# Eighteen products of constants and a new order of issue for a fused attention and expert kernel

## The chip, the cores and the metric

One core of one Trainium2 chip. The metric is the device time of one execution in microseconds (us); the median of three runs counts. The engines are named as in the profile: PE (TensorE, matrix products), DVE (VectorE), ACT (ScalarE), POOL (GpSimd), SP (SyncE, which issues DMAs). Each works through its own queue in order.

## The reference, cut to what matters

Attention over keys and values that are averaged in groups of eight, and after it a layer of eight experts, of which each row of the result goes to one:

```python
k_p = k.reshape(B, H, Sp, pool, D).mean(axis=3)       # B = H = 8, S = 576, pool = 8, D = 64
v_p = v.reshape(B, H, Sp, pool, D).mean(axis=3)
attn = softmax(scale * q @ k_p.T)
x = (attn @ v_p).transpose(0, 2, 1, 3).reshape(B, S, H * D)
...
for b in range(B):                                    # x: (8, 576, 512), F = 1024
    for s in range(S):
        fresh_e = argmax(x[b, s] @ w_gate)
        e = fresh_e if s == 0 or sigmoid(x[b, s] @ w_local) < 0.5 else prev_e
        out[b, s] = p[e] * (relu(x[b, s] @ w1[e]) @ w2[e])
```

## The kernel before

Everything up to the first blocks of the expert layer is one static sequence of small steps, written out in three lists, `PLAN`, `PLAN_B` and `PLAN_C`. A token such as `sc:4` is a step and the number of the unit, load or block it works on; `do` (in the printed code below) turns it into instructions, in the order of the lists. As each engine's queue is in order, the lists fix every engine's order, and the order of SP's DMAs too.

Attention works on four pairs of batches, five units each (`units`, 20 in all). The tokens:

- `lk`, `lv`, `lq` issue the loads of keys, values and queries on SP. There are three buffers for keys (`kk`), three for values (`vt_in`), four for queries (`qt`). `kp` sums groups of eight keys on DVE. `vp` sums values, on POOL or with `.d` on DVE, `vt` transposes them on PE, `vc` copies the transpose (ACT), `vl` multiplies it with the gate weights (PE), `vd` and `vm` write the results into the tile `vaug` (DVE; `vm` on POOL, with `.d` on DVE).
- `sc` is a unit's scores (PE, L458 and L464, for the fifth unit of a pair L473); the tile `sp` has one buffer. `mx`, `sb` are row maxima and the subtraction (DVE, L487, L490), `ex` the exponential (ACT).
- `T0` to `T2` transpose the weights on PE (L521), `T0c` to `T2c` copy them out (ACT); `v0` to `v2` are the products with `vaug` (PE, L563), `v0c` to `v2c` their copies. `fs` scales the logits (DVE), `fp` and `fd` the two halves of the rows, each on POOL or DVE (L600), after which `fd` stores them.
- Per pair, `rA`, `rT0` to `rP` choose the expert of each row: small operations on DVE, transposes and small products on PE (L642, L656 to L677), scans on DVE (L647). Then nine `s` scatter row numbers by expert (POOL, L699).
- `ch`, `er` choose the expert with the most rows after two pairs; its weights are loaded (`w1`, `w2`) and split into two parts (`p1`, `p2`: ACT, then DVE with `.d`, else POOL, L211 and L216). `il` loads a block's row numbers, `ga` gathers the rows (DVE, then POOL), `XR`, `X0`, `X1` turn them.
- `PLAN_B`: `L1` and `L2` are the products of a block's two layers (PE, eight and three products each), `h0`, `h1` what lies between (ACT and DVE, L333 to L339), `tb` a table of the blocks that follow (DVE), `M1` and `M2` the same two layers for the next block. `i1`, `i2`, `i3` load row numbers (SP), `g1`, `f1`, `f3` reduce them (DVE, L256 and L297), `f2`, `f4` gather. `es`, `so` scale and store a block.
- PE writes transposes into the tile `tp` of the pool `ps_t`, which has two buffers. `wa` is three products of the identity, written before the kernel's first data is there.

After `PLAN_C` comes code with branches, `l1_two`, `rest` and `blocks`, with the same instructions before and after the change.

Of the kernel before, what the change touches and what calls it, by code (L numbers as in the profile page):

```python
# [54 lines left out]
PLAN = plan("""
lk:1 lk:0 lv:0 vp:0 lv:1 lq:0 kp:0 lk:2 lv:2 lv:5 lc:0 vm:0 vp:1 wa:0 vt:0 vc:0 kp:1 vp.d:2 sc:0 wa:1 vt:1 lk:3 mx:0
lv:3 vl:0 vt:2 vm:2 vm:1 vp:5 vc:2 vt:5 vd:0 vl:2 sb:0 vd:2 vc:1 vp:3 lq:2 ex:0 lv:6 kp:2 kp:3 lq:1 vl:1 vd:1 vm:3
vc:5 T0:0 vp:6 sc:2 T1:0 T0c:0 v0:0 mx:2 lv:4 lk:5 sb:2 vm:5 T1c:0 vt:3 v0c:0 vc:3 lv:9 v1:0 vp:4 vp:9 lv:8 T2:0 T2c:0
vp:8 vl:3 lq:3 sc:1 ex:2 vd:3 lk:4 lk:6 T0:2 vl:5 vt:4 lv:7 kp:5 lv:11 vc:4 vt:6 vm:6 v2:0 mx:1 v1c:0 lv:10 vd:5 vc:6
T0c:2 T2:2 sb:1 lq:5 v2c:0 fs:0 T1:2 vm:4 T1c:2 v0:2 kp:4 sc:3 kp:6 lq:4 lk:9 vm:8 v0c:2 vt:8 vl:4 fp:0 vd:4 ex:1 vc:8  # L60
T0:1 v1:2 lk:7 T2c:2 v1c:2 T0c:1 vl:6 v2:2 T1:1 T2:1 mx:3 v2c:2 sb:3 lk:10 fd:0 T1c:1 T2c:1 vp:7 ex:3 v0:1 lv:14 T0:3
sc:4 v0c:1 T1:3 fs:2 v1:1 v2:1 T0c:3 vd:6 mx:4 vp:10 T2:3 T1c:3 fp:2 vl:8 vp:11 lv:12 sb:4 kp:7 v1c:1 vt:10 vc:10
v2c:1 sc:5 T2c:3 lq:6 vm:11 kp:10 ex:4 lv:17 mx:5 fd.p:2 vt:7 T0:4 vd:8 fs:1 vc:7 v0:3 v1:3 v0c:3 v2:3 sb:5 lq:7 lk:11
vm:10 vm:9 vm:7 T1:4 fp:1 vl:7 T0c:4 v1c:3 T1c:4 kp:9 vt:11 fd.p:1 lq:12 vd:7 vt:9 vc:11 ex:5 sc:6 T0:5 vp:12 v2c:3
T0c:5 vl:11 mx:6 v0:4 T2:5 vp:17 v0c:4 sb:6 vc:9 v0:5 lv:16 v1:4 T1:5 lq:8 T1c:5 vp:14 v1c:4 fs:3 sc:7 kp:11 vd:11
lv:13 ex:6 fp:3 v1:5 T2c:5 vt:12 T0:6 fd.p:3 vl:9 T0c:6 vc:12 v0c:5 v1c:5 T1:6 lv:19 fs:4 T1c:6 T2:6 rA:0 v2:5 vd:9
rT0:0 mx:7 lk:12 rS0:0 vl:10 sb:7 rT1:0 T2c:6 v2c:5 lq:10 rS1:0 vm:14 fp:4 rT2:0 fs:5 vp:13 ex:7 vd:10 fd.p:4 sc:8
fp:5 lq:9 lk:8 rS2:0 vm:12 mx:8 T2:7 v0:6 T0:7 rE:0 lv:15 rL:0 T0c:7 sb:8 v0c:6 v1:6 v1c:6 T1:7 v2:6 fd.p:5 rO:0 sc:9
rR:0 T2c:7 rV:0 kp:8 T1c:7 vp:19 vt:13 pf:0 ex:8 v2c:6 v0:7 lq:11 vc:13 vp:16 T0:8 mx:9 rP:0 T0c:8 sb:9 vm.d:17 vt:14
vl:12 lv:18 lk:13 v1:7 vd:12 vc:14 vp:15 T1:8 T2:8 sc:10 vm.d:13 ex:9 fs:6 mx:10 lk:15 v0c:7 lq:14 T1c:8 s:0 T0:9 fp:6  # L70
T2c:8 fd.p:6 v1c:7 vl:14 v2:7 v2c:7 v0:8 T0c:9 v0:9 vd:14 vt:15 sb:10 lq:16 s:0 v0c:8 T1:9 T1c:9 vc:15 fs:7 lv:20
sc:11 ex:10 v1:8 v1c:8 s:0 lv:21 s:0 fp:7 T0:10 vm.d:15 vl:13 kp:13 mx:11 kp:12 v2:8 v2c:8 vd:13 v1:9 T1:10 lk:14
vl:15 lq:13 sb:11 vp:18 sc:12 T1c:10 fd.p:7 v0c:9 T2:10 v1c:9 vd:15 fs:8 kp:15 T0c:10 s:0 v0:10 vt:17 ex:11 T2c:10
vc:17 mx:12 sb:12 fp:8 T1:11 fd.p:8 vp:21 T2:11 fs:9 v1:10 T1c:11 vl:17 vm:16 s:0 s:0 rA:1 lv:23 v0c:10 vt:16 v2:10
v1c:10 vc:16 v2c:10 vd:17 fs:10 s:0 T0:11 T2c:11 T0c:11 sc:13 rT0:1 ex:12 rT1:1 rS0:1 vl:16 vd:16 v0:11 vp:20 rS1:1
vt:20 mx:13 rT2:1 rS2:1 fp:9 fp:10 lq:15 rE:1 vc:20 fd.p:10 sb:13 v1:11 rL:1 T1:12 T0:12 T1c:12 s:0 v1c:11 vt:18
v0c:11 rO:1 rR:1 sc:14 vc:18 rV:1 T0c:12 rP:1 v2:11 T2:12 ch:0 vl:18 ex:13 fd.p:9 v0:12 v0c:12 mx:14 lq:19 s:0 kp:14
er:0 s:0 T0:13 v2c:11 vm:21 T2c:12 T0c:13 sb:14 v1:12 T1:13 w2:0 s:0 vt:19 v1c:12 T1c:13 fs:11 vd:18 vp.d:23 w1:0
v2:12 v2c:12 T2:13 s:0 vm:20 s:0 T2c:13 v0:13 lv:22 sc:15 ex:14 fs:12 fp.d:11 vm.d:19 vl:20 fd:11 s:0 w1:1 lq:17 vd:20
fp:12 v1:13 s:0 T1:14 v0c:13 s:0 mx:15 v2:13 sb:15 vc:19 vm.d:23 p1.d:0 vl:19 T0:14 v1c:13 sc:16 v2c:13 vm.d:18 T1c:14  # L80
ex:15 T0c:14 fd.p:12 fs:13 vt:21 vt:23 mx:16 vc:23 vc:21 v0:14 T1:15 T1c:15 vd:19 T0:15 s:0 fp:13 v0c:14 w2:2 v1:14
vl:21 T2:15 v1c:14 fd.p:13 sb:16 sc:17 fs:14 ex:16 vd:21 T0c:15 il:0 rA:2 ga:0 lq:18 p1.d:1 vp:22 T2c:15 vl:23 T2:16
v0:15 rT0:2 rT1:2 mx:17 sb:17 T2c:16 v0c:15 v1:15 vm:22 T0:16 w2:3 rS0:2 v2:15 T0c:16 rT2:2 rS1:2 v1c:15 w1:2 sc:18
rS2:2 fp.d:14 vt:22 vd:23 p2.d:0 fd:14 XR:0 X1:0 rE:2 v2c:15 vc:22 fs:15 fp:15 p2:2 T1:16 vl:22 vd:22 T1c:16 mx:18
v0:16 v1:16 X1c:0 rL:2 ex:17 T0:17 v0c:16 v1c:16 v2:16 sb:18 rO:2 w1:3 T0c:17 il:1 v2c:16 T1:17 sc:19 T2:17 rR:2 fs:16
v0:17 mx:19 T1c:17 rV:2 fd.p:15 fp:16 T2c:17 ex:18 rP:2 v0c:17 T0:18 v1:17 T0c:18 sb:19 fd.p:16 s:0 s:0 T1:18 v2:17
s:0 p1.d:3 v1c:17 T1c:18 T2:18 v2c:17 ex:19 s:0 fs:17 T2c:18 w2:1 fp.d:17 fd:17 s:0 v0:18 T0:19 v0c:18 T0c:19 v1:18
p1.d:2 v1c:18 X0:0 v2:18 X0c:0 T1:19 v2c:18 fs:18 T1c:19 v0:19 v0c:19 v1:19 v1c:19
""")
# [1107 lines left out]
```

## Time and profile before

| | us |
|---|---|
| timed, median of three runs | 643.26 (640.04 to 644.61) |
| profiled execution | 647.41 |
| its span, first to last instruction | 645.6 |
| busy in it: PE | 605.9 (94%) |
| DVE | 433.5 (67%) |
| ACT | 271.0 (42%) |
| POOL | 241.2 (37%) |

The span is made of attention up to about 180 us, the static blocks up to about 238 us, and the blocks with branches after that. Busy times are unions over an engine's instructions; matrix products are pipelined, so two of them overlap in the rows, and a product's start minus that of the one before it is what it costs in a row of products. [...]

### The profile page before, as it was taken

How to read it: one execution, taken by the hardware profiler on the slowest of the kernel's cores; microseconds unless marked ns; L12 is line 12 of the kernel's file. 1: busy time of each engine (PE TensorE's matmuls, PEld its weight loads, DVE VectorE, ACT ScalarE, POOL GpSimd, SP SyncE). 2: the span in 40 equal slices, each digit the busy share in tenths (PEclk: the TensorE clock that was granted, in tenths of full speed). 3: DMA queues.
4: the chain of work that ended last, by engine and by line, in shares of the span. 5: the costliest groups of instructions: out<-in, count | busy, mean ns of one | idle time of the engine just before them, and what ended most of it. 6: DMA issues, size and time to landing. Idle time of an engine off the chain costs nothing. (4 is left out here: it accounts for less than half of the span.)

```text
span 645.6 us, 11811 instructions
## 1 busy us (share of the span) xinstructions
PE 605.9 (94%) x3588; PEld 513.6 (80%) x3588; DVE 433.5 (67%) x1004; ACT 271.0 (42%) x612; POOL 241.2 (37%) x295
## 2 busy tenths in 40 slices
...
GB/s 308 369 291 318 297 271 214 70 268 183 119 67 2 118 298 195 169 101 115 133 75 311 145 112 247 206 192 292 314 174 109 133 58 336 279 200 132 77 82 61
DMA packets 74964, 120.10 MB, mean 186 GB/s; under 512 B 21486, under 2 KB 42994, under 8 KB 74868
## 3 DMA queue, kind: packets, MB, share of 16 engines
...
## 5 line engine op out<-in xcount | busy, mean ns | idle before, releaser
L326 PE MATMUL hp<-x,w1h 128*128 128x512 f32 x376 | 134.5, 398 | 0.0
L347 PE MATMUL o_ps<-w2h,ht_l 128*128 128x512 f32 x312 | 122.5, 392 | 2.4 <-DVE ht_l L339 2.4
L347 PE MATMUL o_ps<-w2h,ht_h 128*128 128x512 f32 x312 | 123.3, 395 | 1.5 <-PEq L1127 0.9
L347 PE MATMUL o_ps<-w2l,ht_h 128*128 128x512 f32 x312 | 121.9, 391 | 1.1 <-DVE w2l L216 1.1
L305 POOL DMA_INDIRECT kk<-x_rows,mi x44 | 44.1, 1003 | 191.1 <-DVE mi L301 172.3
L328 PE MATMUL hp<-x,w1l 128*128 128x256 f32 x376 | 105.6, 281 | 0.0
L333 ACT COPY hs<-hp 128x256 f32<-128x256 f32 x94 | 34.7, 371 | 147.0 <-PE hp L328 145.7
L326 PEld LDWEIGHTS hp<-x,w1h 128*128 128x128 f32 x376 | 70.6, 188 | 17.4 <-DVE hs L334 0.3
L563 PE MATMUL op<-vaug,aT 128*128 128x148 f32 (+5 forms) x448 | 71.6, 321 | 1.7 <-ACT osb L372 1.7
L328 PEld LDWEIGHTS hp<-x,w1l 128*128 128x128 f32 x376 | 71.0, 189 | 1.2 <-DVE w1l L211 0.4
L347 PEld LDWEIGHTS o_ps<-w2h,ht_l 128*128 128x128 f32 x312 | 58.7, 188 | 16.5 <-DVE ht_l L339 3.2
L338 ACT ACTIVATE ht_h<-hs 128x256 fp32r<-128x256 f32 x136 | 56.9, 420 | 34.2 <-DVE hs L334 31.0
L347 PEld LDWEIGHTS o_ps<-w2h,ht_h 128*128 128x128 f32 x312 | 58.8, 189 | 14.6 <-ACT ht_h L959 2.0
L563 PEld LDWEIGHTS op<-vaug,aT 128*128 128x128 f32 (+1 forms) x448 | 65.2, 191 | 6.5 <-ACT osb L372 2.4
L347 PEld LDWEIGHTS o_ps<-w2l,ht_h 128*128 128x128 f32 x312 | 58.9, 189 | 12.7 <-DVE w2l L216 1.4
L339 DVE SCALAR_TENSOR_TENSOR ht_l<-hs,ht_h 128x256 fp32r<-128x256 f32 x136 | 56.7, 417 | 3.4 <-ACT ht_h L338 3.0
L1062 POOL DMA_INDIRECT out<-ob,mi x22 | 28.2, 1284 | 76.2 <-DVE ob L1059 28.3
L334 DVE TENSOR_TENSOR hs<-hp,hs 128x256 f32<-128x256 f32 x94 | 38.7, 418 | 25.9 <-ACT hs L333 24.9
L1059 DVE TENSOR_SCALAR ob<-o_ps,ms 128x512 f32<-128x512 f32 x22 | 16.5, 749 | 51.5 <-PE o_ps L347 49.6
L699 POOL DMA_INDIRECT ids<-pm,pos x36 | 38.0, 1054 | 19.4 <-DVE pos L696 10.9
L1062 POOL DMA_INDIRECT out<-vt_in,mi x20 | 22.5, 1125 | 59.3 <-DVE vt_in L1059 19.3
L319 ACT CAST x<-qt 128x512 fp32r<-128x512 f32 x40 | 24.0, 611 | 42.7 <-DVE qt L314 42.7
...
## 6 DMA issues: line engine op xcount, KB each, us to landing
...
```

Source lines behind the costliest of these rows:

```text
L305: nc.gpsimd.indirect_dma_start(out=xg[b % 2][:, h, :], out_offset=None, in_=x_rows[0:NT + 1], in_offset=bass.IndirectOffsetOnAxis(ap=mi[b ...
L319: nc.scalar.copy(out=xt[:, cs, 0, :], in_=xr_t[:, cs, :])
L326: nc.tensor.matmul(out=ps, lhsT=W1[0][:, kk, f * P:(f + 1) * P], rhs=xt[:, kk].rearrange("p i n -> p (i n)"), start=(kk == 0), stop=False, ...
L328: nc.tensor.matmul(out=ps[:, 0:2 * P], lhsT=W1[1][:, kk, f * P:(f + 1) * P], rhs=xt[:, kk, 0, :], start=False, stop=(kk == KD - 1), skip_g ...
L333: nc.scalar.copy(out=hb[:, 0, :], in_=ps[:, 2 * P:])
L334: nc.vector.tensor_tensor(out=hb[:, 1, :], in0=ps[:, 0:2 * P], in1=hb[:, 0, :], op=ALU.add)
L338: nc.scalar.activation(out=ht[0][:, f, :], in_=hb, func=AF.Relu)
L339: nc.vector.scalar_tensor_tensor(out=ht[1][:, f, :], in0=hb, scalar=0.0, in1=ht[0][:, f, :].bitcast(F32), op0=ALU.max, op1=ALU.subtract)
L347: nc.tensor.matmul(out=to[h], lhsT=ht[i][:, kk, h * P:(h + 1) * P], rhs=W2[j][:, kk, :], start=(n == 0), stop=(n == 3 * KF - 1))
L563: nc.tensor.matmul(out=out, lhsT=lhs, rhs=rhs if len(out.shape) == 3 else rhs.rearrange("p s x -> p (s x)"), start=all(x[0] != n for x in ...
L699: nc.gpsimd.indirect_dma_start(out=ids[u % 4].rearrange("t m w -> (t m) w"), out_offset=bass.IndirectOffsetOnAxis(ap=pos[:, u:u + 1], axis=0),
L1062: nc.gpsimd.indirect_dma_start(out=outv, out_offset=bass.IndirectOffsetOnAxis(ap=mi[b % NM][:, h:h + 1], axis=0), in_=ob[b % 2][:, h, :], ...
```

## The change

A step `wf` (`fill`) is added: one fp32 product of a 128 by 128 tile of ones with 256 columns of ones, into a buffer of `tp` that nobody reads. Eighteen stand in the new `PLAN`. All three lists are replaced. They hold the same steps as before, in another order; eight of them, from `g1` to `M2:1` and `L2:15`, move from `PLAN_C` to `PLAN_B`, and `p2:3` from `PLAN_B` to `PLAN`. Some steps change their engine between DVE and POOL.

```diff
 PLAN = plan("""
-lk:1 lk:0 lv:0 vp:0 lv:1 lq:0 kp:0 lk:2 lv:2 lv:5 lc:0 vm:0 vp:1 wa:0 vt:0 vc:0 kp:1 vp.d:2 sc:0 wa:1 vt:1 lk:3 mx:0
-lv:3 vl:0 vt:2 vm:2 vm:1 vp:5 vc:2 vt:5 vd:0 vl:2 sb:0 vd:2 vc:1 vp:3 lq:2 ex:0 lv:6 kp:2 kp:3 lq:1 vl:1 vd:1 vm:3
-vc:5 T0:0 vp:6 sc:2 T1:0 T0c:0 v0:0 mx:2 lv:4 lk:5 sb:2 vm:5 T1c:0 vt:3 v0c:0 vc:3 lv:9 v1:0 vp:4 vp:9 lv:8 T2:0 T2c:0
-vp:8 vl:3 lq:3 sc:1 ex:2 vd:3 lk:4 lk:6 T0:2 vl:5 vt:4 lv:7 kp:5 lv:11 vc:4 vt:6 vm:6 v2:0 mx:1 v1c:0 lv:10 vd:5 vc:6
...
-vl:21 T2:15 v1c:14 fd.p:13 sb:16 sc:17 fs:14 ex:16 vd:21 T0c:15 il:0 rA:2 ga:0 lq:18 p1.d:1 vp:22 T2c:15 vl:23 T2:16
...
+wa:0 lq:0 lk:1 wf:0 kp:1 lv:0 lk:0 wf:1 wf:2 vp:0 lv:1 wf:3 wf:4 wf:5 wa:1 vp:1 wf:6 vm:0 kp:0 wf:7 wf:8 lv:2 vp.d:2
+wf:9 sc:0 vt:0 lq:2 lc:0 mx:0 lv:5 vp:5 vc:0 sb:0 wf:10 lk:3 wf:11 lv:3 vt:2 lv:4 vt:1 vc:2 wf:12 vl:0 sc:2 vd:0 lv:6
+vl:2 lk:2 vc:1 wf:13 lq:1 vm.d:1 vm.d:2 kp:3 ex:0 vd:2 T0:0 T2:0 vp:3 vl:1 vm:5 lv:8 T2c:0 vd:1 vp:6 mx:2 T1:0 T0c:0
+sb:2 v0:0 T1c:0 wf:14 kp:2 v1:0 ex:2 vt:6 vm.d:3 lv:7 vt:3 vc:6 lk:5 sc:1 vp:4 vp:8 vp:7 lq:3 vm:4 mx:1 vc:3 v1c:0
...
+kp:5 T1c:2 fp:0 lk:6 wf:15 T2:2 sc:3 v1:2 ex:1 vm:7 T2c:2 v0c:2 vc:4 vl:4 T0:1 vp:9 mx:3 v2:2 sb:3 T0c:1 lq:6 v1c:2
...
+lq:8 lv:15 wf:17 v1:4 mx:6 T2:5 vp:14 vl:9 T1c:5 sb:6 T2c:5 lk:10 lv:16 v0c:4 vm:10 v1c:4 kp:11 fs:4 sc:7 ex:6 vt:10
+vd:9 vp:12 T0:6 fp:4 vc:10 fd.p:4 fp:3 lq:9 T0c:6 v0:5 T2:6 vp:15 T2c:6 mx:7 pf:0 vl:10 T1:6 vt:12 rA:0 T1c:6 v1:5
+sb:7 v0c:5 vc:12 rT0:0 vm:12 rS0:0 v2:5 fd:3 v1c:5 rT1:0 rS1:0 rT2:0 v2c:5 rS2:0 sc:8 rE:0 lv:17 ex:7 vd:10 rL:0 kp:9
+T1:7 rO:0 T0:7 fs:5 v0:6 rR:0 T1c:7 lq:11 mx:8 sb:8 rV:0 v0c:6 T0c:7 rP:0 T2:7 vm:14 v1:6 vm:15 lv:18 vm:13 vt:14 ex:8
...
+T1:14 s:0 vc:20 p1.d:0 vl:20 v2c:13 fs:13 vm:18 T0:14 T0c:14 sc:16 ex:15 T1c:14 T1:15 vd:20 s:0 w1:1 fd.p:12 wf:18
+vl:19 T1c:15 mx:16 T0:15 sb:16 T0c:15 vt:21 il:0 fp:13 vd:19 fd:13 p2.d:2 v0:14 vc:21 v1:14 vt:23 v0c:14 w2:3 v1c:14
+vl:21 T2:15 vd:21 sc:17 fs:14 ex:16 vc:23 T2c:15 ga:0 vp:22 rA:2 T0:16 v0:15 rT0:2 T0c:16 mx:17 v0c:15 rT1:2 sb:17
...
 PLAN_B = plan("""
...
-h0:6 s:0 h0:7 tb:6 tb:7 L2:11 s:0 fd:18 s:0 h1:6 s:0 fd:19 s:0 h1:7 L2:12 i2:0 L2:13 L2:5 M1:0 p2.d:3 i1:0 M1:1 M1:2
-L2:14 M1:3 f1:0 L2:6 f2:0 M1:4 L2:7 i3:0 qr:2
...
+fp.d:19 L1:7 L2:11 h0:7 L2:4 h1:6 L2:5 fd:19 X1:1 h1:7 X0c:1 L2:6 L2:12 X1c:1 fd:18 L2:7 es:1 M1:0 M1:1 so:1 i1:0 M1:2
+g1:0 i2:0 f1:0 L2:13 M2:0 f2:0 M2:1 L2:14 L2:15 i3:0 M1:3 f0:0 YR:0 qr:2 M1:4
 """)
 PLAN_C = plan("""
-es:1 g1:0 M1:5 M2:0 M2:1 f3:0 f4:0 ld:0 L2:15 M2:2 M1:6 M1:7 YR:0 es:0 M2:3 M2:4 so:1 M2:5 M2:6 Y1:0 M2:7 so:0 Y0:0
-M2:8 e1:0 M2:9 M2:10 qr:3 M2:11 M2:12 M2:13 i4:0 f0:0 M2:14 M2:15
+es:0 M1:5 M1:6 f3:0 so:0 M2:2 ld:0 f4:0 M1:7 M2:3 M2:4 M2:5 M2:6 i4:0 Y0:0 M2:7 e1:0 Y1:0 M2:8 M2:9 qr:3 M2:10 M2:11
+M2:12 M2:13 M2:14 M2:15
 """)
...
+        def fill():
+            tp = ps_t.tile([P, 512], F32, name="tp")
+            nc.tensor.matmul(out=tp[:, 0:2 * P], lhsT=ones, rhs=ones[:, 0:1].broadcast_to([P, 2 * P]), start=True, stop=True)
...
+            elif op == "wf":
+                fill()
```

## Rows read from the trace of the kernel before

**Rows 1.** Windows: us, busy us (x instructions) per engine, PEclk, DMA share, GB/s
```profile
28.00:66.00 38.00, 36.81 (x360) 33.03 (x360) 33.23 (x67) 20.93 (x54) 28.93 (x45) 1.00 0.90 309
...
82.00:140.00 58.00, 53.42 (x505) 47.93 (x503) 54.82 (x140) 30.19 (x78) 40.91 (x47) 0.97 0.59 189
...
180.00:238.00 58.00, 52.33 (x269) 42.51 (x268) 37.43 (x148) 19.96 (x50) 26.45 (x26) 0.97 0.33 96
238.00:645.60 407.60, 395.70 (x1961) 330.82 (x1959) 245.09 (x479) 163.40 (x348) 90.63 (x83) 1.00 0.53 172
```
**Rows 2.** Windows inside single stretches of the granted clock, columns as above (PE first)
```profile
10.00:27.50 17.50, 16.34 (x88) 14.27 (x89) 10.72 (x19) 3.36 (x9) 15.79 (x25) 1.00 1.04 350
...
72.20:78.90 6.70, 6.19 (x35) 5.68 (x36) 4.75 (x13) 1.66 (x5) 4.94 (x7) 0.50 0.73 256
...
157.60:164.20 6.60, 5.81 (x23) 5.64 (x24) 4.95 (x13) 4.06 (x8) 6.09 (x6) 0.50 0.72 223
...
229.30:232.50 3.20, 3.08 (x12) 2.53 (x12) 0.69 (x1) 1.39 (x3) 1.49 (x2) 0.50 0.97 237
```
**Rows 3.** Timeline of PE: start us, us, line, operation, shapes, count [idle before]
```profile
1.53 1.65 PE L746 MATMUL rt<-ident 128*128 128x128 f32 x6 [1.53 <-POOL ident masks.py:199]
...
10.62 1.17 PE L458 MATMUL sp<-kdz,qt 128*128 128x144 f32 x4
11.72 2.84 PE L464 MATMUL sp<-kd,qt 64*128 64x72 f32 x24
...
62.73 1.56 PE L464 MATMUL sp<-kd,qt 64*128 64x72 f32 x24
...
77.01 2.32 PE L563 MATMUL op<-vaug,aT 128*128 128x148 f32 x8
...
84.80 1.34 PE L563 MATMUL op<-vaug,aT 128*128 128x148 f32 x8
```
**Rows 4.** DVE to 32 us: waits (us, times, longest), then its timeline
```profile
DVE vaug L433 <- PE rt L425: 3.3, 2, 2.3
DVE vs L385 <- DMA vt_in<-in_v: 3.2, 1, 3.2
DVE mx L487 <- PE sp L464: 2.2, 2, 2.0
...
31.94 1.42 DVE L487 TENSOR_REDUCE mx<-sp 128x12 f32<-128x864 f32 x2
```
**Rows 5.** Timeline of DVE where it waits, 66 to 82 us and at 150 us
```profile
76.86 1.42 DVE L487 TENSOR_REDUCE mx<-sp 128x12 f32<-128x864 f32 x2 [1.85 <-PE sp L464]
...
81.08 0.29 DVE L666 TENSOR_TENSOR oh<-rt,iota 128x72 f32<-128x72 f32 x1 [1.46 <-PE rt L661]
...
150.15 0.18 DVE L256 TENSOR_REDUCE idm<-idn 128x4 f32<-128x16 f32 x1 [2.10 <-DMA idn<-ids]
```
**Rows 6.** Waits of PE, then of DVE, 180 to 240 us: us, times, longest
```profile
PE o_ps L347 <- DVE ht_l L339: 2.4, 1, 2.4
PE tp L642 <- DVE ab L627: 1.3, 1, 1.3
PE o_ps L347 <- DVE w2l L216: 1.1, 1, 1.1
...
DVE ids L297 <- DMA idp<-ids: 7.0, 2, 4.5
```
**Rows 7.** Timeline, 205 to 240 us: SP's first index load, DVE's last wait for one, block 0's scaling
```profile
212.56 3.11 SPq L293 DMA_DIRECT2D idp<-ids  x4
...
225.97 0.26 DVE L297 TENSOR_REDUCE ids<-idp 128x16 f32<-128x64 f32 x1 [4.51 <-DMA idp<-ids]
...
238.16 0.75 DVE L1059 TENSOR_SCALAR ob<-o_ps,ms 128x512 f32<-128x512 f32 x1 [3.40 <-PE o_ps L347]
```
**Rows 8.** Timeline of DVE, 194 to 196.5 us: one split, one half of rows
```profile
194.17 1.22 DVE L216 TENSOR_TENSOR w2l<-vt_in,w2h 128x1024 fp32r<-128x1024 f32 x1
...
195.93 0.69 DVE L600 TENSOR_TENSOR xs<-osb,rr 128x512 f32<-128x512 f32 x1
```

More of the change, by code (lines that the diff above doesn't have):

```diff
@@ L61 @@
[L61 to L80, printed above, removed]
```

36 lines of the change are left out of this document (25 added, 11 removed).

## Prediction

> **What bounds the kernel now.** I read the busy times by stage first. From 238 us to the end PE is busy 395.7 of 407.6 us [rows 1]: that part is bound by PE itself, its code isn't touched, and it is shifted as a whole. What can change is the moment at which the last M2 product of the static part ends, now just ahead of 238.16 us, where DVE's scaling of block 0 stops waiting for it [rows 7]. Before that, two stages are nearly full: PE is busy 36.8 of 38 us from 28 to 66 us, and DVE 54.8, PE 53.4 of 58 us from 82 to 140 us. The loss is at the edges: in the first 28 us, around the routing steps of each pair, and in the static block, 180 to 238 us, where PE is busy 52.3 of 58 us [rows 1].
>
> Second, the granted clock. The windows show 0.50, the 1.2 GHz level, in 72.2 to 78.9, 157.6 to 164.2 and 229.3 to 232.5 us [rows 2]. The column reads 1.00 for 10 to 27.5 us too, but the durations contradict it: 24 score products that take 1.56 us at 62.7 took 2.84 us at 11.7 [rows 3]. So I read 10 to 27.5 us as the 1.2 GHz level as well. PE was busy 16.3 us there [rows 2]; at 2.4 GHz up to half of it, 8.2 us, falls away.
>
> Third, who waits at the front. Up to 32 us DVE stands 3.2 us for a load and 3.3 and 2.2 us for PE [rows 4], 8.7 us in all, and after that it is one of the two full engines. PE's half rate delays work that can't be caught up later.
>
> [...]
>
> **The change, term by term.** Both plans hold the same steps but for `wf`, of which the diff has 18 (0 to 15, 17 and 18), not nineteen.
>
> *Price of a fill.* No row has one. Eight v records of 148 columns took 2.32 us at half level and 1.34 us at full [rows 3]. A fill is one fp32 product, two such records of 256 columns: 2 × 256/148 × 2.32/8 = 1.00 us at half level, 0.58 us at full. The lower bound is zero, where PE waits anyway.
>
> *Front (wf:0 to wf:14 and the early tokens).* wa:0 ends at 1.53 + 1.65 = 3.18 us, and PE does almost nothing until sc:0 at 10.62 us [rows 3]. Into that gap go ten fills and wa:1. Ahead of 79 us, where the level was full again, PE had run v products for 2 us [rows 2, 3], and the first six fills are a run of that kind, with 128 rows. [...] sc:0's inputs still come in about as now: lk:0 moves from second to fourth in the queue, but kp:1 goes ahead of kp:0 on DVE, so DVE has work until it lands. [...] sc:2 stands five PE steps earlier, runs at full level too, and vt:3 no longer follows a half-rate v0:0, so most of the 5.5 us of DVE's waits on PE go; lv:2 lies behind five large loads instead of six. I take 4.0 of the 8.7 us. Bounds: +8.2; and if the level never rises, ten fills at 1.00 and 1.65 for wa:1 put sc:0 at 14.8 us, −4.2.
>
> *Routing of pair 0.* In 66 to 82 us DVE waits 1.85 us for sc:8 at half level and 1.46 us for the products of rL:0 [rows 5]. The new order puts v2:5 between rT0 and rT1, T1:6, vt:12 and v1:5 ahead of rT0, and kp:9 on DVE ahead of rO:0, so each side has work while the other's is under way. I take 2.5 of 3.3 us; bounds 0 and 3.3.
>
> *First gather.* ga:0 stood 2.10 us on DVE for the rows of il:0 [rows 5]. il:0 now goes out 20 tokens ahead of ga:0 instead of two. That wait goes, and with it perhaps the low level that follows, whose 5.8 us of PE work cost 2.9 us extra [rows 2]. I take 2.0; bounds 0 and 5.0. Late next is rT1:2, behind rT0:2 and DVE's scan.
>
> *Static block.* PE waits 2.4, 1.3 and 1.1 us, and the low level after the 2.4 costs half of 3.1 us [rows 2, 6]: 6.3 us. es:1, so:1, g1, M2:0, M2:1 and L2:15 move ahead of M1:3, and p2:3, for which the 1.1 us were, leaves this stretch. Against it, i1 and i2 now stand directly before g1 and f1, which need them, so DVE stands there, and behind it wait M1:3's operations, for whose buffer M1:6 waits. Cover on PE between M1:2 and M1:6: L2:13 to L2:15, M2:0, M2:1 and M1:3 to M1:5, 39 products at 52.33/269 = 0.195 us [rows 1], 7.6 us. The index loads take from 212.56 us (issue) to 225.97 us (third used) now [rows 7], two of them about 9 us. fd:18 and fd:19 go out ahead of i1 in either order. I take 3.5, a little over half; bounds −7.3 (under C) and 6.3.
>
> *Engine moves.* Four vm and three fp go to DVE and as many away from it, fd six to it and two away, p2 one and two: 4 × 0.69 − 1.22 = +1.5 us on DVE [rows 8], hidden in DVE's waits at the front, where the vm ones land; if not, −1.5. Loads that change places I cost at nothing, behind the buffers that wait full; if not, the 3.2 us of the one load wait again.
>
> *Later fills, unknown waits.* wf:15 and wf:17 fall where PE is full: −1.2 us. wf:18 falls near 140 us, ahead of a stretch with waits: 0, or −0.6. Any order has waits of its own; 82 to 140 us lose 4.6 us of PE now [rows 1], and I charge about half as new, −2.5; bounds ±4.6.
>
> Sum: 4.0 + 2.5 + 2.0 + 3.5 − 1.2 − 2.5 = 8.3 us. The profiled execution took 647.41 us around its span of 645.6; the median of the three timed runs, 643.26, is 4.2 below. So 639.1 us if profiled in the same way, and 643.26 − 8.3 = **635.0 us** as timed.
>
> **Rivals.**
> *A: loads bind the front.* The DMA share is 1.04 in 10 to 27.5 us [rows 2], so DVE may trade waits on PE for waits on loads. Against: one DVE wait there is on a load, 3.2 us [rows 4]. Front term 0: 8.3 − 4.0 = 4.3, 639.0 us. Chance 0.18.
> *B: the fills don't do what they say,* and the level stays at 1.2 GHz until v0:0. For: wa:0, 1.65 us of full-height products, did not raise it. Against: the fills run on for 5 us. Front −4.2 instead of +4.0: 0.1, 643.2 us. Chance 0.10.
> *C, the other side: DVE stands on the index loads.* If i1 waits for the last scatter and DVE stands the 13.4 us of all three loads [rows 7] against 7.6 us of cover, M1:6 is 5.8 us late, and a low level after it adds 1.5 as at 229 us [rows 2]. It decides as soon as f1 ends more than 7.6 us after M1:2. 8.3 − 3.5 − 5.8 − 1.5 = −2.5, 645.8 us. For: f1 and f3 stood 7.0 us for such loads [rows 6]. Against: i3 has five PE steps more of cover. Chance 0.17.
>
> **How the numbers follow.** The forecast has 0.55. A measurement of this kernel can tell about 1%, 6.4 us, from no change. The forecast's own range is 628 to 641 us; 0.45 of its chance lies below 636.8, 0.10 above. A splits into 0.05 faster and 0.13 within, as other terms may run to their bounds; B is within; C gives 0.06 within and 0.11 slower, where it meets the lower bound of the front. Faster 0.50, same 0.39, slower 0.11. 627.5 to 645.0 us leaves about 2 in 10 out.
>
> **What would show it.** Right: the score products of sc:0 near 1.6 us; mx:1 starting near 28 instead of 31.94 us [rows 4]; no DVE wait over 1 us for idn ahead of 160 us; the last M2 product near 230 us, and 407 us behind it. Wrong: sc:0 still at 2.84 us (B); DVE waits for vt_in or kk in the first 40 us (A); PE idle for several us ahead of M1:6 (C); new low stretches of the clock between 82 and 180 us.

## The result and the profile after

| | before | after |
|---|---|---|
| timed, median | 641.65 (639.86 to 644.61, 4 executions) | 632.46 (631.25 to 633.65, 4 executions) |
| profiled execution | 647.41 | 631.25 |
| its span | 645.6 | 629.1 |

The ratio is 0.985, with a 95% interval of 0.980 to 0.990: 9.2 us less. Measured again later, the same changed kernel took 636.50 us (633.57 to 639.64, 12 executions) and the kernel before, beside it, 642.23, a ratio of 0.992 (0.989 to 0.995). Over everything timed the medians are 642.39 us (74 executions of before) and 635.90 us (16 of after): 6.5 us, 1.0%. The two medians of the changed kernel lie 4.0 us apart, so a difference between two kernels that weren't timed side by side is uncertain by as much, and the readings below heed that.

The windows of the changed kernel, with the columns of [rows 1]:

```profile
28.00:66.00 38.00, 36.15 (x348) 32.22 (x346) 36.87 (x83) 21.73 (x59) 33.18 (x49) 1.00 1.01 369
82.00:140.00 58.00, 52.67 (x507) 46.00 (x504) 55.64 (x143) 30.23 (x76) 40.97 (x49) 1.00 0.67 225
165.00:222.00 57.00, 54.50 (x297) 44.16 (x297) 38.20 (x153) 20.81 (x52) 30.00 (x29) 0.98 0.35 99
222.00:629.10 407.10, 395.46 (x1960) 330.68 (x1958) 244.90 (x479) 163.13 (x348) 85.54 (x81) 0.99 0.54 174
```

The last line is that of [rows 1] again, 395.5 of 407 us on PE: what was gained lies ahead of 222 us. From 28 to 66 us DVE has gone from 33.2 to 36.9 busy microseconds of 38, and the DMA share from 0.90 to 1.01.

The timeline of PE at the front of the changed kernel, with the columns of [rows 3]:

```profile
1.52 1.65 PE L747 MATMUL rt<-ident 128*128 128x128 f32 x6 [1.52 <-POOL ident masks.py:199]
2.97 4.78 PE L751 MATMUL tp<-ones 128*128 128x256 f32 x12
7.59 0.83 PE L747 MATMUL rt<-ident 128*128 128x128 f32 x6
8.25 1.90 PE L751 MATMUL tp<-ones 128*128 128x256 f32 x8
9.99 0.65 PE L459 MATMUL sp<-kdz,qt 128*128 128x144 f32 x4
10.58 1.56 PE L465 MATMUL sp<-kd,qt 64*128 64x72 f32 x24
```

The first fills start 0.85 us apart. `wa:1` takes half of what `wa:0` took, the fills behind it start 0.43 us apart, and the 24 score products take 1.56 us, where [rows 3] had 2.84. So PE runs at full clock from about 7 us on, and `sc:0` starts 0.6 us earlier than before. Full and half clock are 1.00 and 0.50 of the column PEclk, which gives the granted clock as a share; the trace holds shares alone, so the 1.2 and 2.4 GHz of the prediction are names of these two levels, and no run shows a frequency.

DVE in the changed kernel: its longest waits up to 30 us, then rows of its timeline that answer to [rows 4, 5, 7].

```profile
DVE vs L386 <- DMA vt_in<-in_v: 1.4, 1, 1.4
DVE mx L488 <- PE sp L465: 1.4, 1, 1.4
DVE kd L399 <- DMA kk<-in_k: 1.0, 1, 1.0
...
26.96 1.42 DVE L488 TENSOR_REDUCE mx<-sp 128x12 f32<-128x864 f32 x2 [1.39 <-PE sp L465]
...
137.35 0.18 DVE L257 TENSOR_REDUCE idm<-idn 128x4 f32<-128x16 f32 x1
...
206.03 0.27 DVE L298 TENSOR_REDUCE ids<-idp 128x16 f32<-128x64 f32 x1 [4.30 <-DMA idp<-ids]
...
222.00 0.75 DVE L1066 TENSOR_SCALAR ob<-o_ps,ms 128x512 f32<-128x512 f32 x1 [4.04 <-PE o_ps L348]
```

`mx:1` stands at 26.96 us, 5.0 us ahead of [rows 4]; the wait of `ga:0` is gone; block 0's scaling starts 16.2 us earlier than in [rows 7]. Behind the front, one stretch ahead of the last M2 product is at half clock. Before had four: the three of [rows 2] and one from 106.3 to 109.7 us that the prediction missed. The one that is left lies between 82 and 180 us, where the prediction looked for new ones; before had two there. The windows, first of the changed kernel, then of before:

```profile
164.10:167.40 3.30, 3.30 (x17) 2.57 (x19) 2.45 (x7) 2.39 (x5) 2.83 (x3) 0.50 0.73 294
...
106.30:109.70 3.40, 3.40 (x19) 3.14 (x18) 3.32 (x6) 1.50 (x4) 3.24 (x4) 0.50 0.55 191
```

### The profile page after: what moved, and what is told of

It is laid out like the page before. It is cut to its first block, busy times and chain, and to the rows that moved or that the text cites. A ratio compares the mean times of both kernels' runs of the same rounds, so it can differ in the third digit from the quotient of the medians.

```text
span 629.1 us, 11909 instructions
## 1 busy us (share of the span) xinstructions
PE 600.2 (95%) x3624; PEld 508.2 (81%) x3624; DVE 435.7 (69%) x1006; ACT 270.5 (43%) x612; POOL 236.9 (38%) x293
## 5 line engine op out<-in xcount | busy, mean ns | idle before, releaser
L348 PEld LDWEIGHTS o_ps<-w2h,ht_h 128*128 128x128 f32 x312 | 58.6, 188 | 14.5 <-ACT ht_h L966 2.5
L564 PE MATMUL op<-vaug,aT 128*128 128x148 f32 (+4 forms) x448 | 67.4, 313 | 0.5 <-ACT osb L373 0.5
L348 PEld LDWEIGHTS o_ps<-w2l,ht_h 128*128 128x128 f32 x312 | 58.6, 188 | 11.3
L564 PEld LDWEIGHTS op<-vaug,aT 128*128 128x128 f32 (+1 forms) x448 | 61.0, 182 | 4.8 <-issue 1.9
L340 DVE SCALAR_TENSOR_TENSOR ht_l<-hs,ht_h 128x256 fp32r<-128x256 f32 x136 | 56.8, 417 | 3.3 <-ACT ht_h L339 2.5
L335 DVE TENSOR_TENSOR hs<-hp,hs 128x256 f32<-128x256 f32 x94 | 38.8, 418 | 29.2 <-ACT hs L334 28.3
L1066 DVE TENSOR_SCALAR ob<-o_ps,ms 128x512 f32<-128x512 f32 x22 | 16.5, 748 | 52.5 <-PE o_ps L348 51.7
L1069 POOL DMA_INDIRECT out<-ob,mi x22 | 24.7, 1122 | 73.9 <-DVE ob L1066 33.8
L1069 POOL DMA_INDIRECT out<-vt_in,mi x20 | 22.5, 1127 | 63.7 <-DVE vt_in L1066 23.8
L700 POOL DMA_INDIRECT ids<-pm,pos x36 | 38.8, 1078 | 17.5 <-DVE pos L697 9.2
```

Source lines behind the costliest of these rows:

```text
L335: nc.vector.tensor_tensor(out=hb[:, 1, :], in0=ps[:, 0:2 * P], in1=hb[:, 0, :], op=ALU.add)
L340: nc.vector.scalar_tensor_tensor(out=ht[1][:, f, :], in0=hb, scalar=0.0, in1=ht[0][:, f, :].bitcast(F32), op0=ALU.max, op1=ALU.subtract)
L348: nc.tensor.matmul(out=to[h], lhsT=ht[i][:, kk, h * P:(h + 1) * P], rhs=W2[j][:, kk, :], start=(n == 0), stop=(n == 3 * KF - 1))
L564: nc.tensor.matmul(out=out, lhsT=lhs, rhs=rhs if len(out.shape) == 3 else rhs.rearrange("p s x -> p (s x)"), start=all(x[0] != n for x in ...
L700: nc.gpsimd.indirect_dma_start(out=ids[u % 4].rearrange("t m w -> (t m) w"), out_offset=bass.IndirectOffsetOnAxis(ap=pos[:, u:u + 1], axis=0),
L1069: nc.gpsimd.indirect_dma_start(out=outv, out_offset=bass.IndirectOffsetOnAxis(ap=mi[b % NM][:, h:h + 1], axis=0), in_=ob[b % 2][:, h, :], ...
```

## The experiments

All start from the changed kernel or from the kernel before; a time without a further word is a median over 6 or 12 executions, and the ratio is to the kernel before, timed side by side.

**Two runs without a change.**

> The kernel before, profiled once more. The two profiled executions differ by 16.5 us in span (645.6 and 629.1), the timed medians by 9.2 us. Theory (the low stretches of PE's clock fall differently from execution to execution, and the first profile of the kernel before had more of them than most): span 638 to 642 us with fewer low stretches than four behind 28 us. Rival (a profiled execution of the kernel before is always that long): 645 us and the same four stretches.

The kernel before, profiled again: 639.71 us, span 638.0, `mx:1` at 32.38 us, `L1:0` at 174.03, the last M2 product at 230.02 (179.69 and 237.28 us in the first profile), and two stretches at half clock behind the front instead of four, as the theory had it. So 7.6 of the 16.5 us between the first two profiles' spans lie between two executions of one kernel.

> The changed kernel as it is, beside which the other three are read. Theory: 632 to 633 us at the median, 0.985 of the kernel before; its low stretches lie elsewhere than in the first profile, since they move from execution to execution. The product with the row constants of the routing (lgx, 0.3 us when nothing disturbs it) again takes about 2.9 us near 157 us, because the same split runs on POOL beside it. Rival: that long lgx was an accident of the first execution; then it takes 0.3 us here and L1:0 comes about 2.5 us earlier than 162.8 us.

636.50 us (633.57 to 639.64), ratio 0.992; the profile has `mx:1` at 29.42 us, `L1:0` at 171.67 and the last M2 product at 228.66. The time misses the 632 to 633 us of the theory. So neither first profile may stand for its kernel, and I read all profiles together, by stage. A column is the time from one milestone to the next: starts of units' row maxima on DVE (`mx`), and of `L1:0` and `M2:15` on PE. In brackets stand the microseconds of it at half clock, by the trace's records of the granted clock; the time ahead of the first record counts as half clock, as the durations there say.

| profile | 0 to mx:6 | to mx:11 | to mx:18 | to L1:0 | to M2:15 |
|---|---|---|---|---|---|
| before | 57.4 (27.8) | 42.7 (6.8) | 61.2 (7.2) | 18.4 (3.0) | 57.6 (3.4) |
| before again | 57.8 (27.8) | 37.2 (0) | 62.1 (3.1) | 16.9 (0.3) | 56.0 (3.4) |
| before + ten fills | 54.5 (15.2) | 42.8 (6.8) | 60.2 (2.4) | 17.3 (1.0) | 56.1 (6.8) |
| before + new blocks | 55.1 (22.7) | 42.9 (6.8) | 60.9 (0) | 16.6 (0) | 58.3 (6.8) |
| after | 52.2 (7.1) | 37.9 (0) | 58.1 (0) | 20.2 (3.4) | 52.7 (0) |
| after again | 56.8 (13.9) | 38.0 (0) | 58.2 (0) | 18.7 (0) | 57.0 (6.8) |
| after, no fills | 53.6 (22.1) | 36.8 (0) | 59.2 (0) | 20.4 (3.4) | 55.8 (6.8) |
| after, ten fills | 53.8 (15.1) | 37.6 (0) | 58.1 (0) | 20.2 (3.4) | 56.1 (3.4) |
| after, front fills | 54.9 (7.9) | 38.8 (6.8) | 59.1 (0) | 20.1 (3.4) | 56.2 (6.8) |
| after, narrow fills | 55.0 (27.0) | 38.2 (0) | 58.8 (3.4) | 18.7 (0) | 57.3 (10.2) |
| after, old blocks | 53.1 (7.6) | 38.2 (0) | 58.3 (0) | 18.6 (0) | 56.9 (3.4) |
| split on DVE | 52.8 (4.6) | 38.8 (0) | 58.6 (0) | 17.2 (0) | 53.7 (0) |
| split later | 52.6 (4.5) | 37.0 (0) | 59.3 (3.4) | 16.1 (0) | 56.5 (3.4) |
| split later, loads ahead | 52.4 (5.5) | 40.8 (10.2) | 58.7 (6.8) | 16.0 (0) | 54.1 (0) |

Two columns follow their brackets. In the old order, 37.2 us from `mx:6` to `mx:11` becomes 42.7 to 42.9 where 6.8 us of it are at half clock. And the static block takes 52.7 to 54.1 us in the three profiles without a stretch at half clock, and 55.8 to 58.3 in the eleven with one. Such stretches differ between two executions of one kernel, so a single profile can't tell an order's gain from them.

**The fills.** Taken out of the changed kernel (here and below the first line of the list stands for all):

```diff
-wa:0 lq:0 lk:1 wf:0 kp:1 lv:0 lk:0 wf:1 wf:2 vp:0 lv:1 wf:3 wf:4 wf:5 wa:1
+wa:0 lq:0 lk:1 kp:1 lv:0 lk:0 vp:0 lv:1 wa:1
```

> The changed kernel with all eighteen products of constants taken out; the three lists keep their new order otherwise. Theory (the fills raise PE's clock early, and that is the front gain): sc:0 runs at the 1.2 GHz level again (24 score products in about 2.84 us instead of 1.56), mx:1 starts at 30 to 32 us instead of 27.0 us, and the time is 3 to 5 us above the changed kernel's 632.5 us, about 636.5 us. Rival 1 (the order alone does it; PE would leave the low level early in the new order anyway): within 1 us of 632.5 us, mx:1 near 27 us. Rival 2 (the fills only cost their places in PE's queue): 1 to 3 us faster than 632.5 us.

635.32 us (631.6 to 637.93), ratio 0.989 (0.983 to 0.994). The 24 products of `sc:0` took 2.84 us, the granted clock was 0.50 from 8.4 to 25.5 us, and `mx:1` came at 29.36 us, a little better than the theory's 30 to 32. But without fills the changed order is as good as with them within what these runs can tell. Alone, ten of them behind `wa:0` of the kernel before:

```diff
-vp:1 wa:0 vt:0
+vp:1 wa:0 wf:0 wf:1 wf:2 wf:3 wf:4 wf:5 wf:6 wf:7 wf:8 wf:9 vt:0
```

> The kernel before with ten fills behind wa:0 and nothing else changed: PE idles there anyway. Theory (level early is worth 4 to 5 us in any order): sc:0's 24 products take 1.56 us, mx:1 starts near 29 us instead of 31.9 us, and the time is 2 to 4 us below the 641.7 us of the kernel before. Rival (loads bind the front in the old order, or DVE does): the products are faster, yet mx:1 keeps its place and the time is within 1 us of 641.7 us.

640.98 us (636.56 to 644.42), ratio 0.997 (0.994 to 1.001). The level did rise, and fell again. PE's timeline and the windows of this kernel:

```profile
2.97 5.50 PE L751 MATMUL tp<-ones 128*128 128x256 f32 x20
10.25 0.33 PE L420 MATMUL tp<-ident,vs 128*128 128x128 f32 x1 [1.78 <-POOL vs L381]
...
11.01 2.15 PE L465 MATMUL sp<-kd,qt 64*128 64x72 f32 x24
...
11.80:22.00 10.20, 8.40 (x45) 6.84 (x43) 7.52 (x13) 2.61 (x7) 8.96 (x15) 0.50 1.04 368
```

After the ten fills PE stood 1.78 us for POOL, and from 11.8 to 22 us the granted clock was 0.50. `mx:1` came at 29.02 us, 3 us earlier than in before, but `mx:11` at 97.33 us, between the 100.06 and 95.04 of the two profiles of before. The same first list without fills had `mx:1` at 29.68 us in another run below, with the level up at 22.7 us instead of 27.8, so those 3 us aren't clear of what differs between executions. Then the fills with 8 columns in place of 256, so that PE gets as many instructions but little work:

```diff
-nc.tensor.matmul(out=tp[:, 0:2 * P], lhsT=ones, rhs=ones[:, 0:1].broadcast_to([P, 2 * P]), ...)
+nc.tensor.matmul(out=tp[:, 0:8], lhsT=ones, rhs=ones[:, 0:8], ...)
```

> The changed kernel with each product of constants cut from 256 columns to 8: all eighteen keep their places in PE's queue and their tp buffers, but hardly occupy the engine. Theory (what counts is that they keep PE occupied until its clock is granted in full): as without fills, 635.3 us, with sc:0's 24 products at 2.84 us and mx:1 near 29.4 us. Rival (their places in the queue, which hold later products back, do it): as the changed kernel, 632.5 us.

637.63 us (632.72 to 643.15), ratio 0.990 (0.985 to 0.995). The 24 products of `sc:0` took 2.84 us, and the first stretch at full clock began at 27.0 us, as the theory had it; `mx:1` came at 30.32 us. PE's timeline:

```profile
2.97 2.57 PE L751 MATMUL tp<-ones 128*128 128x8 f32 x12
6.81 1.71 PE L751 MATMUL tp<-ones 128*128 128x8 f32 x8
10.32 2.84 PE L465 MATMUL sp<-kd,qt 64*128 64x72 f32 x24
```

So narrow products in the same places leave the front at half clock up to 27.0 us, and the wide ones lift it at 7.1 us, in the first profile of the changed kernel. Yet even here the stage up to `mx:6` takes 55.0 us, where the kernels with wide fills and the new first list span 52.2 to 56.8. The later fills, left out by threes and by eights (`wf:15`, `17`, `18`; then all from `wf:10` on):

```diff
-kp:5 T1c:2 fp:0 lk:6 wf:15 T2:2 sc:3
+kp:5 T1c:2 fp:0 lk:6 T2:2 sc:3
```

> The changed kernel without wf:15, wf:17 and wf:18. Forecast's pricing (two of them fall where PE is full and cost 0.58 us each): 1 us faster, 631.5 us. Rival (they hold the clock level later on): 1 to 2 us slower, with more low stretches behind 28 us. Rival (hidden in waits of PE): no difference.

636.02 us (632.6 to 639.2), ratio 0.988 (0.984 to 0.993).

> The changed kernel with the first ten products of constants only, those ahead of sc:0. In the old order ten fills ahead of sc:0 raised the clock at 5 us, but it fell again at 11.8 us, inside sc:0, and the time gained 1.4 us at most. Theory (wf:10 to wf:14, between the first small products, hold the level until the v products come): the level falls again between 10 and 20 us, mx:1 starts near 28.5 us instead of 27.0, and the time is 1 to 2 us above 632.5 us. Rival (the new order is dense enough after sc:0): as the changed kernel.

637.78 us (632.06 to 641.65), ratio 0.993 (0.989 to 0.997). Neither can be told from the changed kernel's 636.50 us. In the profile of the ten, PE was at half clock again from 15.1 to 25.3 us, as in the kernel with the fills alone (11.8 to 22.0). In the seven profiles that have wide `wf:10` to `wf:14` too, it stayed, once up, at full clock to 27.6 us or longer: the theory was right about the clock, and the time doesn't show it.

**The order of the static block.** The changed first list with the old second and third (less `p2.d:3`, which the first list holds, and one `s:0` more):

```diff
-L1:0 fs:19 rA:3 L1:2 L1:1 h0:0 s:0 p2.d:1 rT0:3 ...
+s:0 ga:1 L1:0 fs:19 L1:2 L1:1 h0:0 rA:3 h1:0 ...
```

> The changed kernel with the old order of the static blocks, the second and third list (without p2.d:3, which is done earlier now, and with one more scatter, which the first list leaves over). Theory (the new order of the blocks saves about 4 us, as 53.5 instead of 58.4 us from the first L1 product to the last M2 product): 636 to 637 us, and that stretch takes 57 to 58 us again with PE waiting about 2.4 us for ht_l ahead of M2:5. Rival (the stretch is shorter only because the steps ahead of it come earlier): within 1 us of 632.5 us.

637.29 us (633.27 to 640.37), ratio 0.992 (0.989 to 0.996), and 56.9 us from `L1:0` to the last M2 product, with 4.4 us of PE's waiting for `ht_l`. Against the first 632.46 us that would be 4.8 us for the new order, against 636.50 it is 0.8. The reverse, the old first list (with `p2.d:3` at its end) and the new block:

```diff
-s:0 ga:1 L1:0 fs:19 L1:2 L1:1 h0:0 rA:3 h1:0 ...
+s:0 L1:0 fs:19 rA:3 L1:2 L1:1 h0:0 s:0 p2.d:1 rT0:3 ...
```

> The kernel before with the second and third list of the change alone: its own first list, with the split p2:3 on DVE at that list's end and one scatter more ahead of the second list. Theory (the new order of the static block is worth 4.8 us whatever stands ahead of it, as the changed kernel with the old blocks was 4.8 us behind the changed kernel): 636.5 to 638.5 us, ratio about 0.993, L1:0 to the last M2 product 52 to 54 us. Rival (the new order of the block lives on what the new first list leaves it, its loads and splits done early): the block still takes 55 us or more and the time is within 2 us of the kernel before.

647.01 us (641.11 to 650.64), ratio 1.007 (1.003 to 1.010): slower than before. The block takes 58.3 us, as the rival had it, but the time fits neither expectation. PE's longest waits from about 175 to 208 us, first here, then in the second profile of before:

```profile
PE o_ps L347 <- DVE ht_l L339: 2.8, 1, 2.8
PE hp L326 <- DVE hs L334: 1.4, 1, 1.4
```

```profile
PE o_ps L347 <- DVE w2l L216: 1.3, 1, 1.3
```

The new block, fed by the old first list, waits longer for DVE. Its 58.3 us are 1.7 more than the mean of the blocks in the old order; the rest of the 4.8 us its one profile doesn't explain.

**A new wait at 157 us.** In every kernel with the split `p2:3` on POOL in the first list, the stage from `mx:18` to `L1:0` is longer: 18.6 to 20.4 us against 16.6 to 18.4 with the old first list, and 18.6 to 18.7 against 16.6 where nothing in it is at half clock. Rows of DVE's timeline in the changed kernel, then of POOL's:

```profile
157.26 2.90 DVE L584 TENSOR_TENSOR lgx<-osb,rr 128x144 f32<-128x144 f32 x1
163.66 0.31 DVE L584 TENSOR_TENSOR lgx<-osb,rr 128x144 f32<-128x144 f32 x1
...
156.54 1.05 POOL L700 DMA_INDIRECT ids<-pm,pos  x1 [2.52 <-DVE pos L697]
157.62 2.36 POOL L217 TENSOR_TENSOR w2l<-vt_in,w2h 128x1024 fp32r<-128x1024 f32 x1
```

The scaling of the logits takes 2.90 us at 157.26 and 0.31 us at 163.66, for the same shape. The long one starts beside a scatter on POOL and ends 0.2 us after the split that follows the scatter. In the later profile it is the same again, with 2.98 us:

```profile
162.00 2.98 DVE L584 TENSOR_TENSOR lgx<-osb,rr 128x144 f32<-128x144 f32 x1
...
162.43 2.36 POOL L217 TENSOR_TENSOR w2l<-vt_in,w2h 128x1024 fp32r<-128x1024 f32 x1
```

Two ways to take the split away from there, on DVE at its place, and on DVE in the second list:

```diff
-rP:2 ex:18 v2c:16 sc:19 s:0 v1:17 X0c:0 fs:16 p2:3 mx:19
+rP:2 ex:18 v2c:16 sc:19 s:0 v1:17 X0c:0 fs:16 p2.d:3 mx:19
```

> Only p2:3 changes its engine, from POOL to DVE, at its place. Theory (POOL's split holds up DVE's two-input operation): the lgx near 157 us falls from 2.9 us to at most 1.5 us (POOL's scatter still runs beside it), the split costs 1.2 us on DVE, L1:0 starts 0.5 to 1.5 us earlier than in the changed kernel and the time falls by as much. Rival (the stretch comes from the scatter alone, and the split only follows it): lgx stays at 2.5 us or more, and DVE's 1.2 us are added: L1:0 about 1.2 us later, the time about 1 us longer.

631.93 us (630.42 to 633.67), ratio 0.984 (0.980 to 0.988). DVE's timeline, then POOL's:

```profile
159.28 0.31 DVE L584 TENSOR_TENSOR lgx<-osb,rr 128x144 f32<-128x144 f32 x1
...
158.61 1.05 POOL L700 DMA_INDIRECT ids<-pm,pos  x1 [2.55 <-DVE pos L697]
159.97 0.97 POOL L700 DMA_INDIRECT ids<-pm,pos  x1 [0.30 <-issue]
```

The scatter still runs beside it, and the operation takes 0.31 us: it was the split. All seven profiles with this split on POOL have 2.90 to 3.19 us there; in the other seven no scaling of the logits behind 150 us takes over 0.4 us. The stage up to `L1:0` takes 17.2 us.

```diff
-rP:2 ex:18 v2c:16 sc:19 s:0 v1:17 X0c:0 fs:16 p2:3 mx:19
+rP:2 ex:18 v2c:16 sc:19 s:0 v1:17 X0c:0 fs:16 mx:19
...
-fp.d:19 L1:7 L2:11 h0:7
+fp.d:19 L1:7 p2.d:3 L2:11 h0:7
```

> p2:3 leaves the first list and stands on DVE after L1:7 in the second, where DVE and ACT were idle between 194.5 and 197.3 us. Theory (POOL's split held up DVE, and DVE sets the end of the first list): lgx at most 1.5 us, L1:0 1.5 to 2.7 us earlier than in the changed kernel, the last M2 product 1 to 2.7 us earlier: 630 to 631.5 us. Rival one (DVE's lgx had slack): L1:0 within 0.4 us and the time the same. Rival two (the split is late for L2:6 or holds up the h1 steps): L1:0 earlier but the last M2 product not.

631.25 us (629.96 to 633.53), ratio 0.983 (0.979 to 0.987). 16.1 us up to `L1:0`, 2.6 and 4.1 us less than in the two profiles of the changed kernel, the first of which has 3.4 us at half clock there. The last M2 product came 0.3 us later than in the first profile, as rival two had it, and 7.3 earlier than in the later one. Timed beside the changed kernel, the one with the split on DVE and this one are 4.9 and 5.4 us ahead of it on average (95%: 3.3 to 6.5 and 3.8 to 7.1), more than the 0.5 to 2.7 us that I had expected. Of the 7.1 us between the spans of the later profile of the changed kernel and of the last one, 4.2 had arisen by `mx:6`, where both issue the same instructions in the same order. So the wait of 2.6 us at 157 us and its cure are shown; that the cure is worth 5 us is not.

**The loads at the front.** Up to `mx:6` the profiles differ in the clock (13.9 us at half clock in the later one of the changed kernel, 4.5 with the later split) and in the DMA traffic. Windows from 22 to 26 us in before, the changed kernel, and the changed kernel again, columns as above:

```profile
22.00:26.00 4.00, 4.00 (x31) 3.87 (x30) 2.01 (x6) 0.42 (x1) 3.71 (x6) 1.00 1.05 342
```

```profile
22.00:26.00 4.00, 2.86 (x26) 2.36 (x24) 2.60 (x4) 2.21 (x6) 3.69 (x5) 1.00 0.74 223
```

```profile
22.00:26.00 4.00, 2.64 (x16) 2.21 (x15) 2.60 (x4) 1.64 (x5) 3.08 (x4) 1.00 0.63 182
```

The DMA engines, busy throughout in before, are now idle for a quarter to more than a third of the time. PE is idle for part of it too; in before it had no idle time there, at half clock. The timeline of SP in the changed kernel, then of POOL, shows why:

```profile
18.45 1.31 SPq L414 DMA_DIRECT2D vt_in<-in_v  x2
22.50 0.39 SPq L411 DMA_DIRECT2D vt_in<-in_v  x1
22.92 0.47 SPq L395 DMA_DIRECT2D kk<-in_k  x1
...
21.20 1.27 POOL L379 TENSOR_TENSOR t<-vt_in 128x512 f32<-128x512 f32 x1 [1.07 <-DMA vt_in<-in_v]
```

`lv:7` stands until 22.50 us for a buffer of `vt_in`, which POOL's sum from 21.20 to 22.47 us frees, and behind it stand `lk:5` and `lq:3`, whose buffers are free: in the run that follows they go out at 19.60 and 20.23 us. So these two go ahead of it, on top of the later split:

```diff
-ex:2 vt:6 vm.d:3 lv:7 vt:3 vc:6 lk:5 sc:1 vp:4 vp:8 vp:7 lq:3 vm:4
+ex:2 vt:6 vm.d:3 lk:5 lq:3 lv:7 vt:3 vc:6 sc:1 vp:4 vp:8 vp:7 vm:4
```

> The kernel with the late split on DVE after L1:7 and, beside it, two loads moved ahead of one in SP's queue: lk:5 and lq:3 (576 and 512 KB, whose buffers are long free) now stand before lv:7, which waits 2.7 to 3 us for a buffer that POOL frees, and behind which the DMA engines ran at 160 to 272 GB/s between 22 and 24 us. Theory (the loads bound the front of the changed kernel, and a waiting load in SP's queue leaves the DMA engines idle): 22 to 26 us at a DMA share of at least 0.95 instead of 0.82, mx:3 and the block's L1:0 0.8 to 2 us earlier than with the late split alone (34.2 and 164.9 us), 629.3 to 630.5 us. Rival one (the traffic is only moved, POOL's groups of v come as late as before and set the pace): DMA share up, mx:3 and L1:0 within 0.4 us, 630.5 to 632 us. Rival two (the 631 us of the late split belong to that chip and that loading of the program, since the changed kernel itself was 632.5 us once and 636.5 us once): 634 to 637 us here.

630.08 us (629.37 to 631.96), ratio 0.983 (0.978 to 0.988): the best of all, 11 us less than before. Its window:

```profile
22.00:26.00 4.00, 2.98 (x29) 2.48 (x27) 3.06 (x4) 2.17 (x6) 3.61 (x6) 1.00 1.00 340
```

The gap in the traffic is closed (0.82 with the later split alone), but `mx:3` comes at 34.04 us where it came at 34.19: up to there the loads only moved, as the first rival said. The time lies in the theory's range, but the 1.2 us against the later split alone were measured on another chip and can't be told from its spread. `L1:0` came at 167.93 us, 3.0 later than with the later split alone, which neither had forecast: this profile has 22.5 us at half clock on the way, the other 7.9. That the later split gives 630 to 631 us on two chips speaks against the second rival.

**Taken together.** With the new first list the ratio to before is 0.985 to 0.993, without the fills or with the old block as with both; the fills alone give 0.997, the new block alone 1.007. So the gain belongs to the new first list, its order and its engines; which of its steps bring it no run isolates.

## Why the prediction came out as it did

The forecast of 635.0 us lies between the two measurements of the changed kernel, 632.46 and 636.50, and the sum of 8.3 us between their gains, 9.2 and 5.7 against before, timed beside it. The steps, by the means of the stages in the table; "old" are the four profiles with the old first list, or with the old block:

| term | forecast | profiles, old minus new |
|---|---|---|
| front, up to mx:6 | +4.0, less 1.2 for `wf:15`, `wf:17` | 56.8 (three without fills) − 53.6 (eight with wide fills) = +3.2 |
| routing of pair 0, mx:6 to mx:11 | +2.5 | 41.4 − 38.2 = +3.2 |
| first gather, mx:11 to mx:18 | +2.0 | 61.1 − 58.6 = +2.5 |
| unknown waits | −2.5 | mx:18 to L1:0: 17.3 − 19.6 = −2.3 |
| static block | +3.5 | 56.7 − 55.8 (six behind the new first list, split as changed) = +0.8 |
| sum | 8.3 | 7.4 |

That the sum came out so near is in part luck: the largest error, 2.7 us too much for the static block, is made good in the main by small errors the other way.

*Front: the size was right, a part of its working wasn't.* I priced a fill at 1.00 and 0.58 us; it costs 0.85 and 0.43. The eight records that I scaled aren't all of 148 columns: the row of [rows 3] names the first one's shape. By shape, in the same stretch of before:

```profile
L563 PE MATMUL op<-vaug,aT 128*128 128x222 f32 x4 | 1.7, 567 | 0.0
L563 PE MATMUL op<-vaug,aT 128*128 128x148 f32 x2 | 0.7, 455 | 0.0
```

By their starts in the trace, a record of 222 columns takes 0.37 us at half clock, and 2 × 256/222 × 0.37 = 0.85: in proportion to the columns, as I had assumed, but from the right shape. At these prices `sc:0` started 0.6 us earlier than before, and its 24 products took 1.56 us. How long a run of products has to last until the level rises, no row of before shows, and the 4.0 us assumed that it rises ahead of `sc:0`. It rose at 7.1 us, and in the other kernels with wide fills at 4.5 to 7.6 us.

Clock and order both have a part in the stage, by the brackets of the table. With about as long at half clock, the new order is ahead of the old by 2.4 to 2.8 us (27 us), 1.5 (22 us) and 0.7 (15 us), and six of the new order's profiles that have 4.5 to 7.9 us at half clock take 53.0 on average, 2.0 less than the one with 27.0. These are single profiles, and the times show no gain from the fills at all. That DVE and the DMA engines are too full then (DVE 36.9 of 38 us busy, DMA share 1.01) for a faster PE to do more than wait is likely, and not shown. The bound of 8.2 us that the rows allowed is 1.3% of the time. The ten fills alone gave 0.3% (−0.1 to 0.6), though they held the level up only from 5.0 to 11.8 us.

*Rival A: its signs are there, its price isn't.* Waits of DVE for `vt_in` and `kk` take 1.4 and 1.0 us, and 2.0 us each in the later profile. But in before DVE stood 3.2 us for `vt_in`, and 4.3 in its second profile, so loads hold it up no more than they did; and the stage did get shorter. I had costed the moved loads at nothing "behind the buffers that wait full". The SP queue, in order, opens a gap in the traffic there, but closing it moved `mx:3` by 0.15 us. In the later profile the gap was followed by 6.8 us at half clock, from 27.6 us on, and `mx:3` came at 38.56 us instead of 33.83. Of the 4.0 us between 632.46 and 636.50 the mean clocks of the executions, 0.990 and 0.986, make 1.4 us at the price below; the rest stays open, since each of the other executions left only a time and a mean clock.

*First gather: right.* The wait of `ga:0` is gone, and the stage came out 0.5 us better than forecast. The clock doesn't explain it: the one old profile with nothing at half clock there takes 60.9 us, the new ones 58.1 to 59.3.

*Routing of pair 0: right in size, but not by the mechanism that I gave.* The two waits of [rows 5], 1.85 and 1.46 us, are gone. But in the second profile of before they are nearly gone as well, from 60 to 96 us:

```profile
DVE oh L666 <- PE rt L661: 0.4, 1, 0.4
DVE mx L487 <- PE sp L464: 0.3, 1, 0.3
```

That execution has no stretch at half clock there, though PE waits as long ahead of it (1.0 us for DVE's scan in both), and its stage of 37.2 us is as short as the new order's 36.8 to 38.8 without one. So the waits that I priced come with the stretch of [rows 2]; the two other profiles of the old list that have it show 1.8 and 1.9 us for the products of `rL:0`. The stretch is there in three of the four profiles of the old first list and in two of the ten of the new one; whether the order makes it rarer can't be told from so few. Where it is there, the new order loses less by it: 38.8 and 40.8 us, where the old takes 42.7 to 42.9.

*Unknown waits: right in size by luck, and they have a name.* I had taken 2.5 us from the time that PE loses between 82 and 140 us, and there it loses 5.3 us now instead of 4.6. What the change did bring lies behind that: most of it is one operation at 157 us, held up by a split that the change had put on POOL. The engine moves were costed by what they add on DVE (+1.5 us), not by what POOL's own instructions do to DVE.

*Static block: the term that was mis-sized.* Only the first profile has 52.7 us; five others with both new lists take 55.8 to 57.3, as the old order does. The waits that I had expected to go were replaced by like ones: PE still stands 2.4 us for `ht_l`, in three pieces, in the first profile, and 3.3 us in one piece for `ht_h` in the later one, ahead of a stretch at half clock that the first doesn't have. With the later split `L1:0` was 3.5 us ahead of the first profile of after, and the last M2 product 0.3 us behind it; that block has 3.4 us at half clock. The two others that moved the split reached 53.7 and 54.1 us, without such a stretch. So short and long blocks part by whether the clock falls in them; that the fall, and not the wait ahead of it, makes the length isn't shown. Every block in the old order has such a stretch, and against the new blocks that have one too, 55.8 to 57.3 us, its 56.0 to 57.6 show no gain. Whether the new order makes the fall rarer stays open.

*Rivals B and C did not happen.* B: the level rose, at 7.1 us. C came near its point: the first index reduction `f1` ended at 206.92 us, 7.3 us after `M1:2` on PE, against the 7.6 us of cover, and `M1:6` started without a gap at 207.30 us.
